# Two residual sums of the last output tiles on GpSimd instead of VectorE

## The chip, the cores and the metric

The kernel runs on one core of one Trainium2 chip. The metric is the device time of one execution, in microseconds (us). Before the change it is 711.5 us, the median of three runs (711.32 to 712.13).

## What is computed

One block of a network for 2048 tokens of width 1024, in bf16: layer normalisation, a local attention with 32 heads (8 positions, two apart), a gated MLP of width 3584, and a gated residual:

```python
x = A_x
xn = _layernorm(x, axis=-1)
s = _A_ref(xn, A_wqkv, A_wo)                  # attention, then a product with wo (1024 x 1024)
g = _silu(_B_ref(xn, B_w1, B_w3, B_w2))       # silu of the gated MLP's output
return x + s * g
```

The last line is what the change touches: for each output tile the product with the gate (`s * g`), then the sum with the input (`x + ...`), then the store.

## The kernel before, in words

The 2048 tokens are worked in two blocks of 1024, each of two chunks of 512 (c = 0 to 3). A chunk has four row tiles of 128 tokens (st = 0 to 3) and two column halves of 512 (dh = 0 and 1). For each block come the projections q, k, v, the MLP's two layers and, for each chunk, the attention and the product with `wo`. The products are done by a scheme of seven half-size products instead of eight, so that sums and differences of operands and partial results are made on VectorE and ScalarE.

Everything is written as operations of a planner (`Plan`). `plan.op(engine, name, emit, reads, writes, occ, lat, late)` gives an operation's engine, the cells that it reads and writes, the time that it should occupy its engine (`occ`) and the time to its result (`lat`). The planner takes the order of TensorE as written, works a due time for every other operation back from it (`limits`), and simulates the engines (`simulate`): of the operations that are ready on an engine, the one with the earliest due time comes next. `late` shifts a due time. The order that results is the order in each engine's queue; an engine works its queue strictly in order. SP's queue holds the loads and the stores. An operation that waits for others does so through semaphores, also where both are on one engine.

The lines of the profile are mostly those of helpers: L433 is every matmul of `mm`, L442 every two-input operation on VectorE (`tt`), L447 every copy from PSUM on ScalarE (`cp`), L456 every DMA (`dma`).

The last chunk (c = 3) has its own order, in `wo(3, wots, True)` (L1477 to L1538). Its output tile in SBUF is `ot`, its input tile `xt`, its gates lie in `xs`. For each tile:

- the matmuls add up the tile in PSUM (`c12`, `c22`, `c21`, `c11`)
- VectorE adds a partial result to it (`oc12`, `oc22`), or ScalarE copies it (`oc21`, `oc11`, `cp`), into `ot` in bf16
- `finish` (L1430) issues the product with the gate (`s_g`), the sum with the input (`x_o`), both two-input operations of 128 x 512 bf16 from SBUF to SBUF on VectorE, and the store from SP's queue
- the very last tile, (0, 1), goes through `final` in two halves of 256 columns; the second is multiplied straight from PSUM and stored from ScalarE's queue

The order of the last tiles is (dh, st): (1, 2) and (1, 0), (1, 1), (1, 3), then the tile (0, 3) of the chunk before, which `flush` brings in, then (0, 2), (0, 0), the first half of (0, 1), (0, 3), the second half of (0, 1). In the trace all of these names read `r` (the buffers of the pool `r8`): `r<-mm,k` is `oc12` or `oc22`, `r<-r,xs` is `s_g`, `r<-r,r` is `x_o`, and `r<-mm,xs` is the product of the last half.

GpSimd issues DMAs in the earlier parts of the kernel and makes constants at its start; it has no arithmetic in the last chunk.

Of the kernel before, what the change touches and what calls it, by code (L numbers as in the profile page):

```python
# [14 lines left out]
PE, DVE, ACT, POOL, SP = range(5)  # L15
# [291 lines left out]
def kernel(  # L307
# [11 lines left out]
    nc = tc.nc  # L319
# [5 lines left out]
    CH = 512  # L325
# [48 lines left out]
    plan = Plan()  # L374
# [5 lines left out]
    for name, pool in (("k2", const), ("mm", psum)):  # L380
# [10 lines left out]
        out=ident[:], in_=ident[:], compare_op=ALU.not_equal, fill=1.0,  # L391
# [4 lines left out]
        out=maskb[:], in_=maskb[:], compare_op=ALU.is_ge, fill=-1.0e9,  # L396
# [14 lines left out]
    def bank(name):  # L411
        return plan.slot("mm", name)
# [27 lines left out]
    def tt(name, fn, o, a, b, rd, wr, n, fast, late=0.0):  # L440
        occ = n / (1920.0 if fast else 960.0) + 0.068
        plan.op(DVE, name, lambda: fn(out=o(), in0=a(), in1=b()), rd, wr, occ, 0.08, late=late)  # L442

    add, sub, mul, mx = (nc.vector.tensor_add, nc.vector.tensor_sub, nc.vector.tensor_mul, nc.vector.tensor_max)

    def cp(name, o, a, rd, wr, occ=0.48):
        plan.op(ACT, name, lambda: nc.scalar.copy(out=o(), in_=a()), rd, wr, occ, 0.11)  # L447
# [5 lines left out]
    def dma(eng, name, o, a, rd, wr, kb, run=1024, late=0.0):  # L453
        e = {SP: nc.sync, POOL: nc.gpsimd, ACT: nc.scalar}[eng]
        occ = {SP: 0.45, POOL: 0.58, ACT: 0.55}[eng]
        plan.op(eng, name, lambda: e.dma_start(out=o(), in_=a()), rd, wr, occ, 0.0, nbytes=kb * 1024, late=late, run=run)  # L456
# [17 lines left out]
    def h_cells(fl, row, gs=range(4)):  # L474
        return [("h", f, row, g) for f in fl for g in gs]
# [27 lines left out]
    def xrow(xt, st):  # L503
        return xt.ap().rearrange("p (s d) -> p s d", s=NST)[:, st, :]
# [446 lines left out]
    def flush():  # L951
        while pend:
            pend.pop(0)()
# [188 lines left out]
    def gate(c, dh, g):  # L1142

        u = c % 2
        if c >= 2:
            i = dh * NST + g
            return (lambda: xsb[:, 2 * u + i // 4, i % 4, :]), [("xs", 2 * u + i // 4, i % 4)]
        if c == 0 and dh == 0:
            return (lambda: xsb[:, 3, g, :]), [("xs", 3, g)]
        fl = (8 if c == 0 else 20 + 4 * dh) + g  # L1150
        return (lambda: h_sb[:, fl, 0:CH]), h_cells([fl], 0)

    def gates(c, dh, g, n):

        if c >= 2:
            return xsb[:, 2 * (c % 2) + dh, g:g + n, :]
        if c == 0 and dh == 0:
            return xsb[:, 3, g:g + n, :]
        fl = (8 if c == 0 else 20 + 4 * dh) + g
        return h_sb[:, fl:fl + n, 0:CH]  # L1160
# [213 lines left out]
    def wo(c, wots, last=False):  # L1374
# [35 lines left out]
        if c == 0:  # L1410
            xa, oa = (lambda: h_sb[:, 12:16, :]), (lambda: h_sb[:, 16:20, :])
            xall = h_cells(range(12, 16), 0) + h_cells(range(12, 16), 1)
        else:
            xt, ot = plan.slot("r8", f"xr{c}"), plan.slot("r8", f"o{c}")
            xa, oa = [lambda t=t: t.ap().rearrange("p (s d) -> p s d", s=NST) for t in (xt, ot)]
            xall = [xt]
        dma(SP, "xr", xa, lambda: x_flat[c * CH:(c + 1) * CH, :].rearrange("(s p) d -> p s d", p=P), [], xall, 1024, 2048)

        def xo(dh, st):
            return lambda: oa()[:, st, dh * CH:(dh + 1) * CH]  # L1420

        def xc(dh, st):
            return h_cells([16 + st], dh) if c == 0 else [(ot, dh, st)]

        def store(dh, sts, late=0.0):
            g0, rows = c * CH, range(NST)[sts]
            dma(SP, "out", lambda: out_flat[g0:g0 + CH, dh * CH:(dh + 1) * CH].rearrange("(s p) d -> p s d", p=P)[:, sts],
                lambda: oa()[:, sts, dh * CH:(dh + 1) * CH], [y for st in rows for y in xc(dh, st)], [], len(rows) * 128, 1024, late)

        def finish(dh, st, n, late=0.0, out=None):  # L1430
            cc = [y for k in range(n) for y in xc(dh, st + k)]
            gc = [y for k in range(n) for y in gate(c, dh, st + k)[1]]
            rows = lambda s: s()[:, st:st + n, dh * CH:(dh + 1) * CH]
            tt("s_g", mul, lambda: rows(oa), lambda: rows(oa), lambda: gates(c, dh, st, n), cc + gc, cc, n * CH, True, late)
            tt("x_o", add, lambda: rows(oa), lambda: rows(oa), lambda: rows(xa), xall + cc, cc, n * CH, True, late)
            if out is None or out:
                store(dh, out or slice(st, st + n), late)

# [2 lines left out]
        def p1(i):  # L1441
            pa[i] = bank(f"sa{c}_{i}")
            mm(pa[i], ow(0, i), wb(0, 0), True, [wots[0]] + owc(0, i), mark=[(pa[i], 0), (pa[i], 1)])

        def p5(i):
            pe[i] = bank(f"se{c}_{i}")
            mm(pe[i], sw(0, i), wt(0), True, sc(0) + wo_tc(0))

        def fork(i):
            pb[i] = bank(f"sb{c}_{i}")  # L1450
            cp("ofork", pb[i].ap, pa[i].ap, [pa[i]], [pb[i]])

        def v5(i):
            sp5[i] = plan.slot("k2", "os5")
            cp("os5", lambda: f32(sp5[i]), pe[i].ap, [pe[i]], [sp5[i]])

        def c11(i):
            mm(pa[i], ow(1, i), wb(1, 0), False, [wots[0]] + owc(1, i))

        def u2(i):  # L1460
            mm(pb[i], sw(1, i), wt(1), False, sc(1) + wo_tc(1))
            su2[i] = plan.slot("k2", "ou2")
            cp("ou2", lambda: f32(su2[i]), pb[i].ap, [pb[i]], [su2[i]])

        def c22(i):
            mm(pb[i], sw(2, i), wt(2), False, sc(2) + wo_tc(2))
            tt("oc22", add, xo(1, i + 2), pb[i].ap, lambda: f32(sp5[i]), [pb[i], sp5[i]], xc(1, i + 2), 512, False)

        def c12(i):
            mm(pe[i], sw(3, i), wb(1, 1), False, sc(3) + [wots[1]])  # L1470
            tt("oc12", add, xo(1, i), pe[i].ap, lambda: f32(su2[i]), [pe[i], su2[i]], xc(1, i), 512, False)
# [5 lines left out]
        if last:  # L1477
            half = lambda a, h: a[:, h * 256:(h + 1) * 256]
            ha = [bank(f"sa{c}_1{h}") for h in range(2)]

            def halves(lhs, rhs, first, rd, hs=range(2)):
                for h in hs:
                    def emit(h=h):
                        for k, (l, r) in enumerate(zip(lhs, rhs)):
                            nc.tensor.matmul(ha[h].ap()[:, :256], lhsT=l(), rhs=half(r(), h), start=first and k == 0,  # L1485
                                             stop=not first and k == 3, skip_group_check=True)

                    plan.op(PE, "mm " + ha[h].name, emit, rd, [ha[h]], 4 * 0.1092, 0.0)

            def fork1():  # L1490
                pb[1] = bank(f"sb{c}_1")
                for h in range(2):
                    cp("ofork", lambda h=h: half(pb[1].ap(), h), lambda h=h: ha[h].ap()[:, :256], [ha[h]], [pb[1]], 0.27)

            def final(h):
                halves(ow(1, 1), wb(1, 0), False, [wots[0]] + owc(1, 1), [h])
                ph, o, cc = lambda: ha[h].ap()[:, :256], lambda: half(xo(0, 1)(), h), [(ot, 0, 1, h)]
                gv, gc = gate(c, 0, 1)
                rows = slice((c * NST + 1) * P, (c * NST + 2) * P)
                if h:  # L1500
                    tt("s_g", mul, o, ph, lambda: half(gv(), h), [ha[h]] + gc, cc, 256, False, 4.0)
                else:
                    cp("oc11", o, ph, [ha[h]], cc, 0.27)
                    tt("s_g", mul, o, o, lambda: half(gv(), h), cc + gc, cc, 256, True, 4.0)
                tt("x_o", add, o, o, lambda: half(xrow(xt, 1), h), [xt] + cc, cc, 256, True, 4.0)
                dma((SP, ACT)[h], "out", lambda: out_flat[rows, h * 256:(h + 1) * 256], o, cc, [], 64, 512)


            p1(0)
            p5(0)  # L1510
            pend.pop(0)()
            fork(0)
            v5(0)
            u2(0)
            halves(ow(0, 1), wb(0, 0), True, [wots[0]] + owc(0, 1))
            fork1()
            c22(0)
            finish(1, 2, 1, out=False)
            p5(1)
            v5(1)  # L1520
            c12(0)
            finish(1, 0, 1, 0.5, slice(0, 4, 2))
            u2(1)
            c12(1)
            finish(1, 1, 1, 1)
            c22(1)
            finish(1, 3, 1, 1.5)
            flush()
            c21(0)
            finish(0, 2, 1, 2)  # L1530
            c11(0)
            cp("oc11", xo(0, 0), pa[0].ap, [pa[0]], xc(0, 0))
            finish(0, 0, 1, 2.5)
            final(0)
            c21(1)
            finish(0, 3, 1, 2.5)
            final(1)
            return  # L1538
# [169 lines left out]
```

## Time and profile before

| | |
|---|---|
| median of three runs | 711.5 us (711.32 to 712.13) |
| the profiled execution | 711.58 us |
| its span, first to last instruction | 709.8 us |
| TensorE's granted clock in it | 1.0 |
| busy: TensorE, VectorE, ScalarE, GpSimd | 700.4, 687.3, 412.1, 38.6 us |
| last matmuls, start | 705.14 us |
| last operations of VectorE, start | 706.51 us |

The profile is of one execution, on the hardware. Times count from the start of the span; what lies around the span (711.58 - 709.8) is start and end of the program. A row of the timeline has start, length, engine, line, operation, output and inputs with their shapes, and how many operations were merged (x2); a bracket tells how long the engine sat idle ahead of it and what ended that. PE is TensorE, DVE VectorE, ACT ScalarE, POOL GpSimd; SPq is SP's DMA queue. Matmuls are pipelined, and their ends are modelled.

### The profile page before, as it was taken

To read this page: it belongs to the slowest core of one execution; us is meant where nothing else is said; L and a number is where in the kernel's file an instruction comes from. 1 tells how busy PE (TensorE), PEld (TensorE's weight loads), DVE (VectorE), ACT (ScalarE), POOL (GpSimd) and SP (SyncE) were. 2 spreads that over 40 slices of the span, in tenths; PEclk is the share of its full clock that TensorE was granted. 3 is DMA by queue.
4 is the path that set the end of the run, shared out by engine and by line. 5 is a ranking of instruction groups with operands and counts; after the bars stand their busy time and mean duration, and the time that the engine had idled before them with its cause. 6 is when DMAs were issued, how large, how long until landed. Compare 5 with 4: busy or idle time off the path is not lost.

```text
span 709.8 us, 9917 instructions
## 1 busy us (share of the span) xinstructions
PE 700.4 (99%) x3578; PEld 369.2 (52%) x3634; DVE 687.3 (97%) x959; ACT 412.1 (58%) x763; POOL 38.6 (5%) x78
## 2 busy tenths in 40 slices
PE   8999999999999999999999999999999999999997
PEld 5655555555555544744555555555555554455443
DVE  7997999999999999999999999998999999999987
ACT  7754566668766798622635355668665654431333
POOL 0010111001200000000100000000000000010000
PEclk9999999999999999999999999999999999999999
DMA  9889887568865769795824569969656744547643
GB/s 327 326 312 330 296 291 243 203 202 273 252 212 181 245 212 218 221 275 181 335 77 171 178 193 344 341 246 295 214 174 200 211 169 157 186 133 237 222 151 103
DMA packets 132209, 162.13 MB, mean 228 GB/s; under 512 B 13248, under 2 KB 109120, under 8 KB 126656
## 3 DMA queue, kind: packets, MB, share of 16 engines
q1 hardware_dynamic: 117744, 127.35, 55.7%
q0 software_dynamic: 5824, 31.99, 11.8%
q10 hardware_dynamic: 8592, 2.16, 2.0%
q8 instruction: 28, 0.46, 0.3%
q14 instruction: 21, 0.17, 0.1%
HBM read 112.72 MB, written 38.27 MB: 213 GB/s over the span
## 4 chain that ended last, share of the span: by engine, by line
PE 95%; ACT 2%; DVE 1%; issue 1%; DMA 1%; SPq 0%; DVEq 0%
PE mm L433 85%; PE mm L1026 6%; PE mm L1290 3%; ACT k L531 1%; DVE r L442 1%; DMA r<-in_A_x_dram 1%; ACT k L534 1%; PE mm L585 1%; ACT k L447 0%; ACT mm L447 0%; ACT L537 0%; ACT r L544 0%; ACT k L450 0%; PE mm L1485 0%; SPq L456 0%
## 5 line engine op out<-in xcount | busy, mean ns | idle before, releaser
L433 PEld LDWEIGHTS <-r 128*128 128x128 bf16 (+1 forms) x2064 | 218.0, 108 | 193.8 <-issue 0.2
L433 PE MATMUL mm<-xs,r 128*128 128x512 f16 x1056 | 251.3, 379 | 0.1
L433 PE MATMUL mm<-xT,r 128*128 128x512 bf16 (+1 forms) x968 | 227.7, 369 | 2.1
L447 ACT COPY k<-mm 128x512 f32<-128x512 f32 (+1 forms) x256 | 133.1, 534 | 58.1 <-PE mm L433 46.8
L433 PE MATMUL mm<-r,h_sb 128*128 128x512 bf16 (+1 forms) x693 | 153.5, 379 | 0.6
L433 PEld LDWEIGHTS <-h_sb 128*128 128x128 f16 (+1 forms) x800 | 78.2, 98 | 93.6 <-DVE h_sb L442 0.5
L442 DVE TENSOR_TENSOR att<-att 128x1024 bf16<-128x1024 bf16 (+6 forms) x176 | 103.7, 603 | 3.9 <-ACT att L883 2.8
L447 ACT COPY mm<-mm 128x512 f32<-128x512 f32 (+1 forms) x121 | 62.2, 517 | 52.8 <-PE mm L433 40.9
L442 DVE TENSOR_TENSOR att<-qo,kT 128x2048 bf16<-128x2048 bf16 x64 | 77.5, 1218 | 3.6 <-ACT kT L447 2.9
L450 ACT ACTIVATE k<-k 128x512 bf16<-128x512 f32 x56 | 33.4, 624 | 64.4 <-DVE k L442 64.4
L442 DVE TENSOR_TENSOR att<-E,vT 128x2048 bf16<-128x2048 bf16 x56 | 66.5, 1213 | 0.0
L442 DVE TENSOR_TENSOR r<-r,r 128x256 f16<-128x256 f16 (+7 forms) x99 | 63.1, 651 | 1.1 <-PE mm L433 0.8
L442 DVE TENSOR_TENSOR h_sb<-mm,k 128x1024 bf16<-128x1024 f32 (+1 forms) x56 | 60.9, 1100 | 0.0
L1026 PEld LDWEIGHTS <-r 128*128 128x128 f16 x392 | 38.3, 98 | 28.4 <-DMA r<-s_dram 0.3
L450 ACT ACTIVATE h_sb<-mm 128x512 bf16<-128x512 f32 x60 | 35.9, 600 | 20.1 <-PE mm L433 19.8
L442 DVE TENSOR_TENSOR k<-mm,k 128x1024 f32<-128x1024 f32 (+1 forms) x44 | 44.7, 1022 | 0.8 <-PE mm L433 0.3
L1026 PE MATMUL mm<-xT,r 128*128 128x256 f16 x224 | 42.8, 273 | 0.0
L447 ACT CAST k<-mm 128x512 bf16<-128x512 f32 x56 | 32.4, 585 | 15.9 <-PE mm L433 15.8
L442 DVE TENSOR_TENSOR h_sb<-h_sb 128x1024 f16<-128x1024 bf16 (+3 forms) x51 | 39.1, 794 | 0.0
L442 DVE TENSOR_TENSOR qo<-qo,att 128x2048 bf16<-128x2048 bf16 x32 | 38.9, 1215 | 0.1
L442 DVE TENSOR_TENSOR r<-r 128x1024 f16<-128x1024 bf16 (+2 forms) x64 | 35.9, 567 | 0.0
L442 DVE TENSOR_TENSOR h_sb<-h_sb,k 128x2048 bf16<-128x2048 bf16 x28 | 34.0, 1215 | 0.2 <-ACT k L447 0.2
(109 smaller groups left out, 507.8 us busy)
## 6 DMA issues: line engine op xcount, KB each, us to landing
r<-in_B_w_dram SPq DMA_DIRECT2D x42, 512.0 KB, 5.2
s_dram<-r POOLq DMA_DIRECT2D x14, 1024.0 KB, 5.2
r<-t_dram SPq DMA_DIRECT2D x16, 896.0 KB, 6.3
r<-s_dram SPq DMA_DIRECT2D x14, 1024.0 KB, 5.2
r<-in_B_w_dram SPq DMA_DIRECT2D x12, 896.0 KB, 4.8
r<-in_A_wqkv_dram SPq DMA_DIRECT2D x10, 1024.0 KB, 7.4
h_sb<-in_B_w_dram SPq DMA_DIRECT2D x14, 512.0 KB, 11.0
t_dram<-h_sb POOLq DMA_DIRECT2D x7, 1024.0 KB, 5.2
```

Source lines behind the costliest of these rows:

```text
L433: nc.tensor.matmul(cut(ps.ap()), lhsT=lhs[k](), rhs=cut(rhs[k]()), start=(first and k == 0), stop=(last and k == n - 1), skip_group_check= ...
L442: plan.op(DVE, name, lambda: fn(out=o(), in0=a(), in1=b()), rd, wr, occ, 0.08, late=late)
L447: plan.op(ACT, name, lambda: nc.scalar.copy(out=o(), in_=a()), rd, wr, occ, 0.11)
L450: plan.op(ACT, name, lambda: nc.scalar.activation(out=o(), in_=a(), func=ACTF.Silu), rd, wr, occ, 0.11, table="silu")
L531: plan.op(ACT, f"mean{c}_{st}", lambda i=i, st=st, junk=junk: nc.scalar.activation(out=b16(junk), in_=xrow(xt, st), func=ACTF.Copy, scale= ...
L534: plan.op(ACT, f"var{c}_{st}", lambda i=i, st=st, junk=junk: nc.scalar.activation(out=b16(junk), in_=xrow(xt, st), func=ACTF.Square, bias= ...
L585: nc.tensor.matmul(tp.ap()[:, k * P:(k + 1) * P], lhsT=xrow(xt, st)[:, kt * P:(kt + 1) * P], rhs=ident[:], start=(k == 0), stop=(k == KH - ...
L1026: nc.tensor.matmul(ps.ap()[:, h * 256:(h + 1) * 256], lhsT=lhs[k](), rhs=rhs[k](), start=first and k == 0, stop=False, skip_group_check=True)
L1290: nc.tensor.matmul(ps.ap()[:, col * 256:(col + 1) * 256], lhsT=lhs[k](), rhs=r()[:, k, :], start=first and k == 0, stop=False, skip_group_ ...
```

## The change

`finish` gets a flag `pool`. Where it is set, the sum `x_o` is an operation of GpSimd (`nc.gpsimd.tensor_add`) and not of VectorE. It is entered with an occupation of 1.0 us and 0.1 us to the result, where `tt` has 512 / 1920 + 0.068 = 0.33 us and 0.08 us. Two calls set the flag: tile (1, 3) and tile (0, 2) of the last chunk. Product, store and everything else stay with the same engines and queues.

```diff
-        def finish(dh, st, n, late=0.0, out=None):
+        def finish(dh, st, n, late=0.0, out=None, pool=False):
             cc = [y for k in range(n) for y in xc(dh, st + k)]
             gc = [y for k in range(n) for y in gate(c, dh, st + k)[1]]
             rows = lambda s: s()[:, st:st + n, dh * CH:(dh + 1) * CH]
             tt("s_g", mul, lambda: rows(oa), lambda: rows(oa), lambda: gates(c, dh, st, n), cc + gc, cc, n * CH, True, late)
-            tt("x_o", add, lambda: rows(oa), lambda: rows(oa), lambda: rows(xa), xall + cc, cc, n * CH, True, late)
+            if pool:
+                plan.op(POOL, "x_o", lambda: nc.gpsimd.tensor_add(out=rows(oa), in0=rows(oa), in1=rows(xa)), xall + cc, cc,
+                        1.0, 0.1, late=late)
+            else:
+                tt("x_o", add, lambda: rows(oa), lambda: rows(oa), lambda: rows(xa), xall + cc, cc, n * CH, True, late)
             if out is None or out:
                 store(dh, out or slice(st, st + n), late)
...
             c22(1)
-            finish(1, 3, 1, 1.5)
+            finish(1, 3, 1, 1.5, pool=True)
             flush()
             c21(0)
-            finish(0, 2, 1, 2)
+            finish(0, 2, 1, 2, pool=True)
             c11(0)
             cp("oc11", xo(0, 0), pa[0].ap, [pa[0]], xc(0, 0))
             finish(0, 0, 1, 2.5)
```

In the queues of the built program VectorE's order is that of before with the two sums left out. GpSimd's queue gets the two sums at its end. On SP the store of the chunk before comes ahead of that of (1, 3); the stores of (1, 3) and (0, 2) wait for GpSimd. TensorE's and ScalarE's queues stay as they are.

## The prediction

> **What bounds the kernel now.** I read the page first, then the chain of work that ended last, then the last microseconds by stage and in order of time.
>
> ```profile
> span 709.8 us, 9917 instructions
> PE 700.4 (99%) x3578; PEld 369.2 (52%) x3634; DVE 687.3 (97%) x959; ACT 412.1 (58%) x763; POOL 38.6 (5%) x78
> PE 95%; ACT 2%; DVE 1%; issue 1%; DMA 1%; SPq 0%; DVEq 0%
> ```
>
> Three lines of the page: TensorE bounds the kernel (95% of the chain), VectorE is nearly as busy (97% of the span), GpSimd nearly idle (5%). Since the edit touches only the last output tiles, the shares decide nothing; the end of the chain does. Columns: start in us, length in us, what.
>
> ```profile
> 696.21 4.33 PE mm L433 x20
> 700.63 0.70 DVE r L442
> 701.36 3.04 DVE r L442 x8
> 704.43 2.37 DVE r L442 x8
> ```
>
> The chain leaves TensorE at 700.54 and then follows VectorE to the end. Taken alone, these rows promise a gain: 16 operations back to back on VectorE, two of which are to go. The rows in order of time say whether that backlog reaches the end. First the two hand-over times, then the tail (start, length, engine):
>
> ```profile
> 694.51 0.58 ACT L447 CAST r<-mm 128x512 bf16<-128x512 f32 x1 [0.28 <-PE mm L433]
> 695.13 0.42 DVE L442 TENSOR_TENSOR r<-r,xs 128x512 bf16<-128x512 bf16 x1 [0.39 <-ACT r L447]
> ...
> 697.77 1.03 PE L433 MATMUL mm<-r,h_sb 128*128 128x512 bf16 x4
> ...
> 698.91 0.69 DVE L442 TENSOR_TENSOR r<-mm,k 128x512 bf16<-128x512 f32 x1 [0.19 <-PE mm L433]
> ...
> 702.30 0.42 DVE L442 TENSOR_TENSOR r<-r,r 128x512 bf16<-128x512 bf16 x1
> 702.32 0.58 ACT L447 CAST r<-mm 128x512 bf16<-128x512 f32 x1 [1.98 <-PE mm L433]
> 702.64 0.75 DVE L442 TENSOR_TENSOR r<-r,xs 128x512 bf16<-128x512 bf16 x2
> 703.18 0.58 ACT L447 CAST r<-mm 128x512 bf16<-128x512 f32 x1 [0.28 <-PE mm L433]
> ...
> 703.31 0.75 DVE L442 TENSOR_TENSOR r<-r,r 128x512 bf16<-128x512 bf16 x2
> ...
> 703.98 0.42 DVE L442 TENSOR_TENSOR r<-r,xs 128x512 bf16<-128x512 bf16 x1
> 704.04 0.86 ACT L447 CAST r<-mm 128x512 bf16<-128x512 f32 x2 [0.28 <-PE mm L433]
> ...
> 704.43 0.42 DVE L442 TENSOR_TENSOR r<-r,r 128x512 bf16<-128x512 bf16 x1
> 704.77 0.62 DVE L442 TENSOR_TENSOR r<-r,xs 128x512 bf16<-128x512 bf16 x2
> ...
> 705.14 0.60 PE L1485 MATMUL mm<-r,qo 128*128 128x256 bf16 x4
> 705.31 0.61 DVE L442 TENSOR_TENSOR r<-r,r 128x512 bf16<-128x512 bf16 x2
> 705.34 0.58 ACT L447 CAST r<-mm 128x512 bf16<-128x512 f32 x1 [0.44 <-PE mm L433]
> 705.85 0.41 DVE L442 TENSOR_TENSOR r<-mm,xs 128x256 bf16<-128x256 f32 x1
> 706.18 0.41 DVE L442 TENSOR_TENSOR r<-r,xs 128x512 bf16<-128x512 bf16 x1
> 706.51 0.62 DVE L442 TENSOR_TENSOR r<-r,r 128x256 bf16<-128x256 bf16 x2
> ```
>
> From ScalarE's end to VectorE's start pass 695.13 - (694.51 + 0.58) = 0.04 us; from TensorE's, 698.91 - (697.77 + 1.03) = 0.11 us. Where two adds of 0.42 take 0.75 together, the second starts 0.33 after the first.
>
> Name the products s_g(half, tile), the sums x_o(half, tile). VectorE runs x_o(1,1) at 702.30, s_g(1,3) at 702.64, s_g and x_o of the chunk before at 702.97 and 703.64, x_o(1,3) at 703.31, s_g(0,2) at 703.98, x_o(0,2) at 704.43, s_g(0,0) at 704.77, the first half of the last tile's product at 705.11, x_o(0,0) at 705.31, that half's sum at 705.64; then from 705.85 the product of the second half, straight from PSUM, s_g(0,3), and two sums, ending at 706.72 + 0.41 = 707.13. Against the times at which their inputs are ready, s_g(0,2) is 0.18 us late (ScalarE ends at 703.76, plus 0.04), s_g(0,0) 0.11 us late (704.62 plus 0.04), the product at 705.85 not at all: the last matmuls end at 705.14 + 0.60 = 705.74, plus 0.11 is 705.85. So VectorE has caught up with TensorE when the last product starts, although the chain shows no break there. From 705.85 on nothing is removed.
>
> **The change part by part.**
>
> *The two sums leave VectorE.* x_o(1,3) and x_o(0,2) are 0.42 us each. Both lie ahead of 705.85. Without them s_g(0,2) moves to 703.80 and s_g(0,0) to 704.66, where ScalarE stops them; the last product stays at 705.85 and s_g(0,3) behind it. Removed: 0.84 us of busy time; off the end: 0, at most 705.85 - 705.74 = 0.11 us if the hand-over from TensorE can be shorter than the row shows. What is late next is the last matmul.
>
> *The order.* In the built program VectorE's row is the same with the two taken out; TensorE's and ScalarE's rows are unchanged. On SP's queue the store of the chunk before moves ahead of that of (1,3), and both stores of the moved sums now wait for GpSimd: (1,3), (0,2), then (0,0), the first half of the last tile, and (0,3). SP works in order, so these three wait as well if GpSimd is late. All twelve stores are still issued.
>
> *The two sums on GpSimd.* No two-input operation on GpSimd stands in this trace. The nearest rows:
>
> ```profile
> 0.28 0.10 POOL L1692 MEMSET const-float32-1.0<- 128x1 f32 x1
> ...
> 1.02 0.29 POOL L390 TENSOR_SCALAR_AFFINE_SELECT ident<-ident 128x128 bf16<-128x128 bf16 x1
> ```
> ```profile
> L442 DVE TENSOR_TENSOR r<-r,r 128x512 bf16<-128x512 bf16 x6 | 2.4, 417 | 0.0
> ```
>
> The lower end is VectorE's 0.42 us. The select has a quarter of the columns in 0.29 us: four times that is 1.16 us. For the upper end, I double it for the second input: 2.3 us. I take 1.16, the nearest row in engine and layout. A fixed part, as in the memset of one column (0.10 us), would make it less, the second input more.
>
> *GpSimd beside VectorE.* If they don't touch, the first sum runs from 702.64 + 0.42 + 0.04 = 703.10 to 704.26, the second from 704.26 (its product ends at 703.80 + 0.42 = 704.22) to 705.42. SP's last issues:
>
> ```profile
> 705.79 0.81 SPq L456 DMA_DIRECT2D out_dram<-r  x2
> ...
> 707.19 0.33 SPq L456 DMA_DIRECT2D out_dram<-r  x1
> ```
>
> Two issues take 0.81 us, so 0.4 us each; the store of (0,2) must be issued by 707.19 - 3 x 0.4 = 705.99 if the last is not to be late. At 1.16 us per sum it is (705.48); it would be up to 1.4 us per sum. So, apart, the sums cost 0.
>
> But both engines read the same two SBUF buffers in a stretch in which VectorE has no gap of more than 0.2 us. Whether one must stand while the other reads, no row shows. The bounds are: no interaction, 0; and turns, one instruction of the one or the other at a time. I take the turns. By the rows alone, either end is open: VectorE's two-input adds keep 0.42 us throughout this tail, but with nothing on GpSimd beside them.
>
> The Trainium skill, "SBUF — State Buffer", section "Who interferes with whom", says that a VectorE instruction with two SBUF inputs contends with a GpSimd instruction that reads SBUF, that the one which starts first holds the shared ports for its whole instruction, and that the other blocks fully. By that rule the sum is the one with turns, without it the one at nothing; no run here shows it yet.
>
> *The sum with turns.* The product of the chunk before holds the path until 702.97 + 0.42 = 703.39, and its sum must wait for it anyway; so GpSimd's first sum goes in, 703.39 to 704.55. Then x_o of the chunk before at 704.59, s_g(0,2) at 704.93 to 705.35, s_g(0,0) from 705.26 to 705.68; GpSimd's second sum, ready at 705.39, runs 705.68 to 706.84. Then come the first half's product 706.88, x_o(0,0) 707.08, the half's sum 707.41, the last product 707.62, s_g(0,3) 707.95, sums at 708.28 and 708.49, end 708.90. Against 707.13 that is +1.77 us, nearly two GpSimd sums less the two spacings of 0.33 given back. SP is no second cost: the store of (0,2) goes out at 706.9, the last at 708.96. The landing adds what it adds now:
>
> ```profile
> DMA to landing us min/median/max: 1.6/1.7/1.8
> ```
>
> The profiled execution took 711.58 us, 1.78 more than its span, and lies 0.08 above the median of the three runs (711.5). So 711.5 + 1.77 = 713.27, written as **713.3 us**. Each 0.1 us by which the sum on GpSimd is longer or shorter counts twice: at 0.42 us it gives 711.8, at 1.55 us 714.05, at 2.3 us 715.6. If the read path is free before an add's recorded end (the adds start 0.33 apart but last 0.42), each turn costs some 0.1 less: 713.1.
>
> **The rivals.**
>
> *They don't touch* (not slower): the mechanism is that GpSimd reads beside VectorE. For it: GpSimd has nothing else to do in the tail, its last work before being
>
> ```profile
> 629.19 1.08 POOL L456 DMA_DIRECT2D E<-att  x2 [2.75 <-issue]
> ```
>
> so the two sums end by 705.5. Against it: only the shared-path argument. Time 711.4 to 711.6, a change of -0.11 to 0. It decides as long as a sum takes under 1.4 us; at 1.6 us the store of (0,2) is issued at 706.36 and the last 0.4 us later than now, 711.9.
>
> *VectorE keeps GpSimd out.* Its adds follow each other without a gap, so GpSimd gets in only after 707.13. Then its sums run to 707.13 + 2 x 1.16 = 709.45, and the store of (0,2) and the three behind it on SP go out at 709.5 to 710.7 against 707.19: +3.5, 715.0 us. Against it: the chunk's product and sum are now adjacent and dependent, which opens VectorE's reads around 703.4, and ScalarE holds s_g(0,2) back.
>
> *Only one sum collides*: the second falls beside the product that reads PSUM, or into a wait for ScalarE. Half the price, 712.3.
>
> *The backlog is real*: VectorE's 0.66 us come off the end, 710.9. The rows at 705.74 and 705.85 speak against it. That the sums don't move at all is excluded by the built program.
>
> **How the numbers follow.** Turns 0.58; don't touch 0.28; kept out 0.08; one collides 0.04; real backlog 0.02. A measurement of this kernel can tell about 0.2% from no change: 1.4 us, so faster is below 710.1 and slower above 712.9. Of the turns, spread by the length of a GpSimd sum, I put 0.43 above 712.9 and 0.15 below. Slower: 0.43 + 0.08 = 0.51. Within 0.2%: 0.15 + 0.28 + 0.04 + 0.02 = 0.49, of which 0.01 goes to faster for a gain that I fail to see: 0.48. The range runs from the lower end of "don't touch", 711.3 with the spread of the three runs (711.32 to 712.13), to turns with sums of 1.55 us and some spread, 714.4. It leaves out "kept out", the backlog, and turns above 1.7 us, together under 0.2. The likeliest case alone: 712.3 to 714.1.
>
> **What would show each step.** Length: two two-input adds on GpSimd, 1.0 to 1.4 us each if undisturbed. Turns: VectorE's rows between 703.4 and 707 have holes of about 1.1 us, or single adds of over 1 us, while GpSimd runs; the last product starts near 707.6. Don't touch: that product still starts 0.11 us after the last matmul, and the last store is issued at 707.2. Kept out: GpSimd's sums end after VectorE's last, with four stores bunched behind. I'm wrong if VectorE's adds keep 0.42 us beside GpSimd, if a GpSimd sum is far from 1.16 us, or if the last product starts earlier than 705.85.

## The result, and the profile after

The changed kernel takes 714.79 us (median of five runs, 714.23 to 715.23) against 711.51 us before (five runs, 711.32 to 712.13): a ratio of 1.0045, with a 95% interval of 1.0034 to 1.0056. It is 3.3 us slower. The forecast was slower, at 713.3 us, in a range of 711.3 to 714.4: the sign was right, and the time lies 0.4 us above the range.

The profiled execution took 714.23 us. From its page:

```profile
span 712.4 us, 9978 instructions
PE 703.4 (99%) x3634; PEld 369.3 (52%) x3634; DVE 688.4 (97%) x957; ACT 412.3 (58%) x763; POOL 41.1 (6%) x80
```

VectorE has two instructions fewer and is 1.1 us longer busy. TensorE's 703.4 us against 700.4 is no loss: the trace of before lacks records of matmuls (3578 against 3634, with 3634 weight loads in both). The tail in order of time shows why (start, length, engine; the added rows are those of POOL):

```profile
702.26 0.76 DVE L442 TENSOR_TENSOR r<-r,xs 128x512 bf16<-128x512 bf16 x2
...
702.82 1.20 POOL L1436 TENSOR_TENSOR r<-r,r 128x512 bf16<-128x512 bf16 x1 [72.93 <-PE mm L433]
703.05 1.26 DVE L442 TENSOR_TENSOR r<-r,r 128x512 bf16<-128x512 bf16 x1
...
704.72 1.27 POOL L1436 TENSOR_TENSOR r<-r,r 128x512 bf16<-128x512 bf16 x1 [0.70 <-DVE r L442]
704.77 0.60 PE L1489 MATMUL mm<-r,qo 128*128 128x256 bf16 x4
...
706.60 0.41 DVE L442 TENSOR_TENSOR r<-mm,xs 128x256 bf16<-128x256 f32 x1
706.93 0.41 DVE L442 TENSOR_TENSOR r<-r,xs 128x512 bf16<-128x512 bf16 x1
707.26 0.61 DVE L442 TENSOR_TENSOR r<-r,r 128x256 bf16<-128x256 bf16 x2
```

Between them, in a narrower window of the same timeline, and the same operation before the change:

```profile
704.90 1.23 DVE L442 TENSOR_TENSOR r<-r,xs 128x256 bf16<-128x256 bf16 x1
```
```profile
705.11 0.28 DVE L442 TENSOR_TENSOR r<-r,xs 128x256 bf16<-128x256 bf16 x1
```

One VectorE operation beside each GpSimd sum is stretched: x_o of the chunk before from 0.42 to 1.26 us, the product of the first half from 0.28 to 1.23 us. Each ends 0.1 to 0.3 us after the GpSimd sum that it overlaps (704.31 after 704.02, 706.13 after 705.99). This execution reached its tail 0.37 us earlier than that of before (last matmuls at 704.77, not 705.14), so I count from the end of the last matmul, 705.37. VectorE's last operation ends at 707.87, 2.50 us behind it; before it was 1.39. That is 1.1 us of loss.

The span, though, ends 7.06 us behind the last matmul (712.43), and ended 4.06 us behind it before: 3.0 us of loss. The missing 1.9 us lies behind the last store. It is not in the chain of work nor in the timeline of busy instructions. It is in the view of one source line: the line of the program's end, where engine, operation, count, then shortest/median/longest ns, and first and last start are given. Before:

```profile
L1703 POOLq DRAIN  x3: 40/93/6297, 629.6 to 709.5; - x3
```
```profile
L1703 SPq DRAIN  x3: 7/7/7, 709.0 to 709.3; - x3
```

and after:

```profile
L1707 POOLq EVENT_SEMAPHORE  x4: 17/17/17, 711.7 to 712.3; - x4
L1707 POOLq DRAIN  x3: 40/102/6955, 704.7 to 712.2; - x3
```
```profile
L1707 SPq DRAIN  x3: 7/7/7, 709.7 to 711.9; - x3
```

GpSimd's closing DRAIN stands right behind its last work. Before, it starts at 629.6 us and lasts 6.30 us: over at 635.9, almost 74 us ahead of the end, it delays nothing. After, it starts beside the second sum at 704.7 and lasts 6.96 us, to 711.64: its recorded time takes in the sum that it stands behind, and from the sum's end at 705.99 it is 5.65 us. SP is through with its stores at 709.7 and waits for it; the closing exchange of semaphores, in which every engine takes part, follows at 711.7. The table of waits has the same, under the name of TensorE's queue (us in total, times, longest):

```profile
SPq L1707 <- PEq L1707: 2.5, 2, 2.1
```

Before, the row read 0.6 us in total, 0.5 the longest.

### The profile page after: what moved, and what is told of

It is laid out like the page before. It is cut to its first block, busy times and chain, and to the rows that moved or that the text cites. A ratio compares the mean times of both kernels' runs of the same rounds, so it can differ in the third digit from the quotient of the medians.

```text
span 712.4 us, 9978 instructions
## 1 busy us (share of the span) xinstructions
PE 703.4 (99%) x3634; PEld 369.3 (52%) x3634; DVE 688.4 (97%) x957; ACT 412.3 (58%) x763; POOL 41.1 (6%) x80
## 4 chain that ended last, share of the span: by engine, by line
PE 97%; DVE 1%; DMA 1%; SPq 0%; issue 0%; DVEq 0%
PE mm L433 88%; PE mm L1026 6%; PE mm L1290 3%; DVE r L442 1%; DMA r<-in_A_x_dram 1%; PE mm L585 1%; PE mm L1489 0%; SPq L456 0%; DVE small L512 0%; DVE r L520 0%; PE mm L572 0%; DVEq L1707 0%; DVE small L519 0%; DVEq L442 0%
## 5 line engine op out<-in xcount | busy, mean ns | idle before, releaser
L433 PE MATMUL mm<-xT,r 128*128 128x512 bf16 (+1 forms) x1008 | 232.1, 369 | 0.0
```

The lines of the kernel that those rows point to most:

```text
L433: nc.tensor.matmul(cut(ps.ap()), lhsT=lhs[k](), rhs=cut(rhs[k]()), start=(first and k == 0), stop=(last and k == n - 1), skip_group_check= ...
```

## The experiments

Two theories were open after this trace. **D**: the end waits for GpSimd's DRAIN, which ends some 5.65 us after GpSimd's last work. **T**, the one of the prediction: VectorE's stalls beside GpSimd's sums set the loss. A ratio below is against the kernel before, measured together with it, with its 95% interval. The edits of "One sum at a time" and of "The two sums four microseconds earlier" start from the changed kernel; those with memsets and the copy start from the kernel before.

### One sum at a time

Only (1, 3) moved:

```diff
-            finish(0, 2, 1, 2, pool=True)
+            finish(0, 2, 1, 2)
```

> Only the sum of tile (1,3) is on GpSimd. Theory D (the closing DRAIN of GpSimd ends about 5.65 us after its last work, and the end of the program waits for it): GpSimd's sum ends near 704.4 us of a span like that of before, DRAIN 710.0, span 710.8, time about 712.5 us. Theory T (VectorE's stalls alone set the loss): one stall of 0.84 us less the 0.33 us saved, 712.0 us. The trace tells them apart: under D the last thing before the end is GpSimd's DRAIN, under T the landing of the last store.

Only (0, 2) moved:

```diff
-            finish(1, 3, 1, 1.5, pool=True)
+            finish(1, 3, 1, 1.5)
```

> Only the sum of tile (0,2) is on GpSimd. Theory D: its sum runs 704.5 to 705.8, DRAIN to 711.4, span 712.2, time about 713.9 us, 1.4 us more than with the other tile alone, since the sum lies 1.4 us later. Theory T: one stall of about 0.9 us less 0.33, about 712.1 us, the same as with the other tile alone.

Measured: 712.61 us for (1, 3), ratio 1.0018 (1.0009 to 1.0027), and 713.72 us for (0, 2), ratio 1.0031 (1.0020 to 1.0043). In each, one VectorE row is stretched (1.26 us in both), so T would have them alike, but the later sum costs twice as much. The DRAIN rows with their sums, first (1, 3), then (0, 2):

```profile
703.20 1.21 POOL L1436 TENSOR_TENSOR r<-r,r 128x512 bf16<-128x512 bf16 x1 [72.92 <-PE mm L433]
```
```profile
L1707 POOLq DRAIN  x3: 40/93/6890, 703.2 to 710.6; - x3
```
```profile
704.50 1.15 POOL L1436 TENSOR_TENSOR r<-r,r 128x512 bf16<-128x512 bf16 x1 [74.21 <-DMA out_dram<-r]
```
```profile
L1707 POOLq DRAIN  x3: 40/93/6847, 704.5 to 711.8; - x3
```

For (1, 3) the times of the two theories are close, but the trace has the DRAIN end at 710.1, behind SP's last stores (709.6). Less the sum that it stands behind, the DRAIN is 5.68 and 5.70 us: 6.89 - 1.21 and 6.85 - 1.15.

### A memset that stalls nobody, at two times

All sums are back on VectorE, and GpSimd writes one column of a gate that has been read already:

```diff
             finish(0, 2, 1, 2)
+            gv = lambda: gates(c, 0, 2, 1)
+            plan.op(POOL, "tick", lambda: nc.gpsimd.memset(gv()[:, :, 0:1], 0.0), [], gate(c, 0, 2)[1], 0.1, 0.1)
```

> All sums stay on VectorE, and GpSimd gets one memset of one column (into the gate of tile (0,2), after its product has read it). It reads nothing and lasts 0.1 us. Theory D: it ends near 704.55, DRAIN 710.2, span 711.0, time about 712.7 us. Theory T: nothing stalls VectorE, so 711.5 us. A DRAIN that is long only after an addition would also give 711.5.

The same behind `finish(0, 3, 1, 2.5)`, with the gate of (0, 3):

> As the run with one memset of one column, but into the gate of tile (0,3), after its product, 2.2 us later in the tail; no sum is moved. Theory D: it ends near 706.75, DRAIN 712.4, span 713.2, time about 714.9 us, 2.2 us above the earlier memset. Theory T: 711.5 us.

Measured: 712.79 us, ratio 1.0018 (1.0009 to 1.0026), and 714.85 us, ratio 1.0049 (1.0036 to 1.0063). No VectorE row changes, and a memset of one column costs as much as the whole change when it comes at the end. The memset of the second run, and the two DRAINs, first that of the earlier memset:

```profile
707.29 0.10 POOL L1538 MEMSET xs<- 128x1 bf16 x1 [76.38 <-DVE r L442]
```
```profile
L1705 POOLq DRAIN  x3: 40/93/5772, 704.6 to 710.9; - x3
```
```profile
L1705 POOLq DRAIN  x3: 40/102/5772, 707.3 to 713.6; - x3
```

Both are 5.77 us, 5.67 behind the memset. D holds: what matters is when GpSimd's last work ends, not what it is.

### The two sums four microseconds earlier

```diff
-            finish(1, 2, 1, out=False)
+            finish(1, 2, 1, out=False, pool=True)
...
-            finish(1, 0, 1, 0.5, slice(0, 4, 2))
+            finish(1, 0, 1, 0.5, slice(0, 4, 2), pool=True)
...
-            finish(1, 3, 1, 1.5, pool=True)
+            finish(1, 3, 1, 1.5)
...
-            finish(0, 2, 1, 2, pool=True)
+            finish(0, 2, 1, 2)
```

> The sums of tiles (1,2) and (1,0), about 4 us earlier in the tail, are on GpSimd, those of (1,3) and (0,2) back on VectorE. Theory D: GpSimd's last work ends near 701.5 us, its DRAIN near 707.1, before SP has seen the last store land (709.0), so it costs nothing: 711.5 us. A theory by which a two-input sum on GpSimd costs what it cost here wherever it stands: about 714.5 us. Stalls of VectorE, if any, fall ahead of the last matmul and are caught up.

Measured: 711.24 us against 711.26, ratio 1.0000 (0.9991 to 1.0009). The timeline:

```profile
698.22 1.16 POOL L1436 TENSOR_TENSOR r<-r,r 128x512 bf16<-128x512 bf16 x1 [68.13 <-DVE r L442]
699.96 1.16 POOL L1436 TENSOR_TENSOR r<-r,r 128x512 bf16<-128x512 bf16 x1 [0.58 <-DVE r L442]
```
```profile
698.73 0.69 DVE L442 TENSOR_TENSOR r<-mm,k 128x512 bf16<-128x512 f32 x1 [0.65 <-PE mm L433]
699.46 0.42 DVE L442 TENSOR_TENSOR r<-r,xs 128x512 bf16<-128x512 bf16 x1
700.46 0.69 DVE L442 TENSOR_TENSOR r<-mm,k 128x512 bf16<-128x512 f32 x1 [0.58 <-PE mm L433]
```

```profile
L1707 POOLq DRAIN  x3: 40/102/6845, 699.9 to 709.4; - x3
```

The DRAIN is over at 706.8 and hidden. VectorE is not stalled either: what runs beside the sums has one input in PSUM (`r<-mm,k`) and keeps its 0.69 us. And nothing is gained by taking two sums, 0.84 us, off VectorE, as it has caught up with the last matmul anyway.

### Writing and reading beside VectorE

GpSimd's memset writes the whole gate, 128 x 512:

```diff
+            gv = lambda: gates(c, 0, 2, 1)
+            plan.op(POOL, "tick", lambda: nc.gpsimd.memset(gv(), 0.0), [], gate(c, 0, 2)[1], 0.1, 0.1)
```

> All sums on VectorE; GpSimd writes the whole gate of tile (0,2), 128 x 512, with a memset after its product: it reads nothing. If only GpSimd's reads collide with VectorE's two-input operations, VectorE's rows from 704.4 on keep 0.42 and 0.28 us; if any access collides, one of them grows by the memset's length (about 0.5 us). Theory D gives a span of about 711.4 us and a time near 713.1 us either way.

or copies it onto itself:

```diff
+            gv = lambda: gates(c, 0, 2, 1)
+            plan.op(POOL, "tick", lambda: nc.gpsimd.tensor_copy(out=gv(), in_=gv()), [], gate(c, 0, 2)[1], 0.1, 0.1)
```

> As the run with the memset of the whole gate, but a copy of the gate onto itself: GpSimd reads one input. If its reads collide, one of VectorE's two-input rows behind 704.8 grows from 0.42 us to about the copy's length (0.9 to 1.2 us); if it takes two inputs on GpSimd to collide, they keep 0.42. Theory D gives about 713.6 us either way.

Measured: 712.95 and 713.83 us, one execution each. The memset with VectorE's rows from 704.18 on, then the copy with its own:

```profile
704.21 0.52 POOL L1532 MEMSET xs<- 128x512 bf16 x1 [74.18 <-DVE r L442]
```
```profile
704.18 0.42 DVE L442 TENSOR_TENSOR r<-r,r 128x512 bf16<-128x512 bf16 x1
704.53 0.62 DVE L442 TENSOR_TENSOR r<-r,xs 128x512 bf16<-128x512 bf16 x2
```
```profile
704.74 0.86 POOL L1532 COPY xs<-xs 128x512 bf16<-128x512 bf16 x1 [74.19 <-DVE r L442]
```
```profile
704.71 0.43 DVE L442 TENSOR_TENSOR r<-r,r 128x512 bf16<-128x512 bf16 x1
705.05 1.03 DVE L442 TENSOR_TENSOR r<-r,xs 128x512 bf16<-128x512 bf16 x2
```

Beside the write nothing grows, though only its last 0.20 us lie beside an operation that started after it (704.53 to 704.73). Beside the read the pair takes 1.03 instead of 0.62 us. So what VectorE stands for is GpSimd's reading. The stretch is 0.41 us, less than the 0.86 us of the copy: VectorE's operation at 705.05 starts 0.31 us behind the copy, and the rest of the copy, to 705.60, is what it can have waited for. The expectation, a stretch to the copy's length, was too high. The 0.86 us may themselves hold a wait of GpSimd for the VectorE operation that started at 704.71, just before the copy; no run has the copy alone.

### Where the DRAIN comes from

DMAs by GpSimd are issued from SP's queue instead, with the earlier memset kept:

```diff
-        e = {SP: nc.sync, POOL: nc.gpsimd, ACT: nc.scalar}[eng]
+        e = {SP: nc.sync, POOL: nc.sync, ACT: nc.scalar}[eng]
```

> The memset of one column into the gate of tile (0,2), as before, and every DMA that GpSimd issued (about 68 in all) is issued from SP's queue instead, so GpSimd does nothing but ten short operations at the start and that memset. If the long DRAIN at the end closes what GpSimd's own DMAs left open, it drops from 5.77 us to well under 1 us. If it is a fixed price behind GpSimd's last work, it stays at 5.7 to 5.8 us. The time itself also moves with the DMAs and is not the point of this run.

Then with 32 of the 68 left on GpSimd, those of the attention, and with one:

```diff
+        e = {SP: nc.sync, POOL: nc.gpsimd if name[0] in "LE" else nc.sync, ACT: nc.scalar}[eng]
```

> One memset of one column in the tail, and of GpSimd's 68 DMAs only the 32 of the attention stay on GpSimd, the other 36 go from SP. If the DRAIN grows with the number of DMAs, it takes 2.7 us; if any DMA by GpSimd brings the whole price, 5.7 us and a time near 712.7 us.

```diff
+        e = {SP: nc.sync, POOL: nc.gpsimd if name == "wtp" else nc.sync, ACT: nc.scalar}[eng]
```

> The same memset, and of the 68 DMAs just one (the store of the sums of wo, some 370 us ahead of the end) stays on GpSimd. By number the DRAIN takes 0.3 us; if any DMA by GpSimd brings the whole price, 5.7 us and a time near 712.7 us; if the price goes by the eight semaphore lanes in use, some 0.7 us more than without.

Measured: 711.28, 712.46 and 711.44 us, one execution each. The DRAINs, in this order:

```profile
L1705 POOLq DRAIN  x3: 34/77/183, 703.9 to 709.2; - x3
```
```profile
L1705 POOLq DRAIN  x3: 39/148/2817, 704.6 to 710.4; - x3
```
```profile
L1705 POOLq DRAIN  x3: 34/89/278, 704.0 to 709.4; - x3
```

Less the memset's 0.10 us: 0.08 with no DMA, 0.18 with one, 2.72 with 32, 5.67 with 68. That is a line: 0.08 us and 0.082 us for each DMA that GpSimd issued, whatever its size and even 370 us back (0.08 + 32 x 0.082 = 2.70; 0.08 + 68 x 0.082 = 5.66). The pages of the runs with 68, 32 and one rule out two other measures. Packets, MB and share of what GpSimd issued:

```profile
q0 software_dynamic: 5824, 31.99, 11.8%
```
```profile
q0 software_dynamic: 1536, 4.20, 1.8%
```
```profile
q0 software_dynamic: 144, 2.10, 0.7%
```

Going from 68 to 32 cuts the packets to 26% and the bytes to 13%, but the DRAIN above its 0.08 us to 47%, and 32 of 68 is 47%. The 712.46 us with 32 isn't the DRAIN's doing: it was over at 707.4, two microseconds before SP. What else made that one execution longer isn't known.

### The stalls alone

With the DRAIN out of the way, the price of the stalls can be timed. First the base, all 68 DMAs on SP and no sum moved, then the change on top of it; the edit is the first of the section above, without the memset:

> The kernel before, with GpSimd's 68 DMAs issued from SP's queue and no sum moved. It is the base for the next run. Expected within 0.2% of 711.5 us: the run with these DMAs on SP and one memset took 711.28 us. If it is faster than the kernel before, it is a version that beats both.

> The change as it stands (sums of (1,3) and (0,2) on GpSimd), with GpSimd's 68 DMAs issued from SP's queue, so that the closing DRAIN is short (0.2 us). What is left is the price of the stalls alone. By the trace of the changed kernel VectorE ends 2.50 us behind the last matmul against 1.39 before: 1.1 us above the base of this call, about 712.6 us. A theory in which the stalls are absorbed and the DRAIN was all of the loss gives 0 against the base; the turns as first forecast give 1.8 us.

Measured: 711.78 us, ratio 1.0006 (0.9996 to 1.0015), and 712.78 us, ratio 1.0021 (1.0012 to 1.0030), eleven executions each: the stalls cost 1.0 us, with the executions of either spread over some 1.6 us. VectorE's last rows and the last matmuls with the sums on GpSimd, then in the base:

```profile
704.97 0.60 PE L1489 MATMUL mm<-r,qo 128*128 128x256 bf16 x4
```
```profile
707.50 0.61 DVE L442 TENSOR_TENSOR r<-r,r 128x256 bf16<-128x256 bf16 x2
```
```profile
705.05 0.60 PE L1485 MATMUL mm<-r,qo 128*128 128x256 bf16 x4
```
```profile
706.42 0.62 DVE L442 TENSOR_TENSOR r<-r,r 128x256 bf16<-128x256 bf16 x2
```

VectorE ends 2.54 us behind the last matmul, against 1.39 in the base: 1.15 us, as in the changed kernel (1.11). No version beat the kernel before by more than the spread.

## Why the prediction was right in sign and too small

- **No gain from VectorE's freed time: right.** With two earlier sums moved and no stall, the ratio is 1.0000.
- **Length of a sum on GpSimd, 1.16 us: right, in part by luck.** Measured 1.20 and 1.27 in the changed kernel, and 1.15 to 1.21 with one sum or with the earlier ones. But the figure was four times a select with one input; no run shows that a sum with two inputs had to follow it.
- **Turns between the engines: right, and now shown.** VectorE's two-input operation from SBUF is held while GpSimd reads. The rule of the Trainium skill ("SBUF — State Buffer", section "Who interferes with whom") agrees in its three parts: two inputs in SBUF beside a read stretch (0.42 to 1.26 us), beside a write of 0.52 us they don't, and with one input in PSUM (0.69 us) they don't. GpSimd seems to wait as well: its sum took 1.15 us where VectorE had just stood idle (only (0, 2) moved), and 1.20 and 1.27 us where a VectorE operation still had 0.20 and 0.26 us to run. No experiment was made on that side.
- **The sum with turns, +1.77 us: mis-sized.** The stalls cost 1.1 us by VectorE's end and 1.0 us timed alone. I charged each turn nearly a whole sum on GpSimd. The two stretches are 1.26 - 0.42 = 0.84 and 1.23 - 0.28 = 0.95, together 1.79, less the two spacings of 0.33: 1.13. GpSimd's first sum starts while the product ahead of it still runs (702.82, with the pair recorded to 703.02), and a held operation ends 0.14 to 0.29 us after GpSimd, not a full 0.42.
- **"SP is no second cost": right.** The stores of the moved sums go out well ahead of the last.
- **The end: the step that failed.** "The landing adds what it adds now" took all that follows VectorE's last operation as unchanged. It holds for the landing, but not for the end of the program, which waits for GpSimd's DRAIN as well. The trace of before had it: a DRAIN of 6.3 us behind GpSimd's last DMA at 629.6 (the row above), which the prediction did not use: it read GpSimd's busy operations and not the program's end. With it the sum would have been: the second sum as I placed it to 706.84, plus 5.67, plus 0.8 for the closing exchange, 713.3 us of span, 715.1 us of time. With the turns as measured, the second sum ends at 705.99, 0.62 us behind the last matmul's 705.37, and 0.62 + 5.65 for the DRAIN + 0.79 for the exchange are the 7.06 us to the end of the span.
- **That the number came close was partly luck.** Two errors pull against each other: some 0.7 us too much for the stalls (1.77 against 1.1), and 1.9 us for the DRAIN that was put at nothing. The forecast "slower" owes its size to the DRAIN too: the stalls alone gave 712.78 us, which by the prediction's own bound of 712.9 would not have counted as slower.
- **The rival "they don't touch" was priced wrong for the same reason.** At no contention at all, the second sum would have ended at 705.42, and the DRAIN at 711.1: still over 2 us slower.

What stays open: what the DRAIN does for each DMA. The runs show its length and that it goes by the number of GpSimd's DMAs, not its inside; the runs with 0, 1 and 32 DMAs and a memset are single executions.

## What to carry to other kernels

Before giving an idle engine work at the end of a kernel, look at what that engine does between its last work and the end of the program: here, with 68 DMAs issued by GpSimd, any GpSimd instruction, even of one column, had to end 5.7 us before SP's last store had landed, or every microsecond counted in full. Offloading two-input operations from VectorE to GpSimd is paid back in stalls when VectorE works on two SBUF inputs at that moment; beside operations with one input in PSUM there was no stall. And check the backlog against the inputs' ready times before pricing a relief: a chain that stays on one engine to the end doesn't say that the engine is late.

## What the runs showed of the hardware that I had not expected

- GpSimd's closing DRAIN costs 0.08 us plus 0.082 us for each DMA that GpSimd issued in the whole program (0, 1, 32 and 68 DMAs: 0.08, 0.18, 2.72 and 5.67 us), counted from the end of its last instruction (a sum, a copy or a memset here).
- Issuing all 68 of GpSimd's DMAs from SP's queue changed the time by less than can be told (ratio 1.0006, 0.9996 to 1.0015), and left a DRAIN of 0.08 us behind GpSimd's last work.
- A two-input sum of 128 x 512 bf16 takes GpSimd 1.15 to 1.27 us, a copy 0.86, a memset 0.52, each with VectorE at work beside it for at least part of the time.
